# Attention backward: rings of three single PSUM banks, the dS product per head, half of one unit in four turned by TensorE and evacuated by ScalarE

## The chip, the cores and the metric

One core of a Trainium2 chip runs the whole kernel. The metric is device time in microseconds; for the kernel before it is the median of three runs. The engines are TensorE (PE; its weight loads are shown as PEld), VectorE (DVE), ScalarE (ACT), GpSimd (POOL) and SyncE (SP, which here only issues DMA). Matmul results land in PSUM, which has eight banks of 512 fp32 a partition; DVE and ACT read them out.

## The reference, cut to what matters

A transformer block (layer norm with modulation, attention with 32 heads of width 16 over 2048 positions, an MLP with squared ReLU) is run forward and backward: the outputs are the block's output and the gradients of nine inputs. The part that matters is the gradient of the attention:

```python
q, k, v = (qkv[0], qkv[1], qkv[2])            # H = 32, Dh = 16, S = 2048
scores = jnp.einsum('bhqd,bhkd->bhqk', q, k) * scale
p = _softmax(scores, axis=-1)
o = jnp.einsum('bhqk,bhkd->bhqd', p, v)
...
_out, _vjp = jax.vjp(_f, A_x, A_wqkv, A_wo, B_w1, B_b1, B_w2, B_b2, c, w_mod)
_grads = _vjp(grad_out)
```

With P the probabilities and dO the gradient of o, the backward pass needs dP = dO V^T, dS = P * (dP - rowsum(dO * O)), then dV = P^T dO, dK = dS^T Q and dQ = dS K. The scores are computed again, block by block. The row sums and the division by the softmax's sums are folded into the operands earlier, so that in the loop below dS is one product of dP (in PSUM) and the exponential (in SBUF).

## The kernel before: the attention backward loop

The kernel has a forward stage, this loop, and a last stage with the weight gradients. The loop goes over 8 groups of four heads (`g`), two pairs of heads in each (`jp`), four chunks of 512 keys (`c`) and 16 blocks of 128 queries (`ib`): 1024 units. A unit is one block of queries against one chunk of keys for two heads (`a` = 0 and 1). Units come in fours (G), which share one SBUF tile `ds`.

The eight PSUM banks: two for score tiles (`st`), two tiles of two banks each for dP (`dp`), one accumulator for dK and dV (`acckv`), one for dQ (`accq`).

```python
stp = es.enter_context(tc.tile_pool(name="p5st", bufs=2, space=PSUM))
dpp = es.enter_context(tc.tile_pool(name="p5dp", bufs=2, space=PSUM))
accp = es.enter_context(tc.tile_pool(name="p5acc", bufs=1, space=PSUM))
```

Work on a unit is spread over time. In step i the scores of unit i and the dP of the unit before are multiplied in turn, head by head; the exponential follows per head, the dS product for both heads at once:

```python
for a in range(2):
    stt = stp.tile([P, 512], F32, name="st")
    rs = slice(64 * jp, 64 * jp + 64)
    nc.tensor.matmul(stt[:], lhsT=T["QT"][rs, q], rhs=masked["KT"][2 * jp + a][rs, c0:c0 + 512],
                     start=True, stop=True)
    if last:
        dP(dp, last, a)
    nc.scalar.activation(pu[:, a, :], stt[:], ACT.Exp, scale=self.scale)
if last:
    dS(dp, last)
last = (T, g, jp, c, ib, kvT, pu, dsg, i, grp)
if i % 2 == 1 and len(pend) >= 4:
    r = kv_two()                       # dK, dV of two earlier units
    if r:
        turnq.append(r)
elif i % 2 == 0 and len(pendq) > 2 * G:
    for _ in range(4 if len(pendq) > 3 * G else 2):
        dq(pendq.pop(0), [0, 1])       # dQ of two earlier units
if i == G - 1 and ib0 // G % 2:
    turn_ds(dsg, grp)
```

`dq` needs dS transposed (`dsT`, 32 blocks of 128x128 for four units). A DMA does that when the four units are complete, issued from SP:

```python
def dS(dp, u):
    (T, g, jp, c, ib, kvT, pu, dsg, i, grp) = u
    nc.vector.tensor_tensor(dsg[:, i], dp[:], pu[:], ALU.mult)
    pend.append((T, g, jp, c, ib, kvT, pu, dsg[:, i]))
    if i == G - 1:
        i0 = len(grp)
        dsT = grp[0] if i0 else dtp.tile([P, 8 * G, P], BF16, name="dsT")
        nc.sync.dma_start_transpose(dsT[:, 8 * i0:, :], dsg[:, i0:].rearrange("p i a k -> p (i a k)"))
        for i in range(G):
            pendq.append((T, g, jp, c, ib - G + 1 + i, i, dsT))
```

In every second group of four units the first unit's eight blocks go another way: TensorE transposes them into a score tile, ACT copies half of it out and DVE the other half. The DMA then has 24 blocks to do.

```python
def turn_ds(dsg, grp):
    dsT = dtp.tile([P, 8 * G, P], BF16, name="dsT")
    tp = stp.tile([P, 8, P], BF16, name="st")
    for b in range(8):
        nc.tensor.transpose(tp[:, b, :], dsg[:, 0, b // 4, b % 4 * P:(b % 4 + 1) * P], self.ident[:])
    nc.scalar.copy(dsT[:, 0:4, :], tp[:, 0:4, :])
    nc.vector.tensor_copy(dsT[:, 4:8, :], tp[:, 4:8, :])
    grp.append(dsT)
```

`kv` runs four matmuls for each unit into `acckv`, on four strips of columns; after the sixteenth block DVE moves the sums to `kvT`. At the end of a pair of heads `turn` transposes `kvT` in 16 blocks, in a `dp` tile, and ACT copies the result out.

Of the kernel before, what the change touches and what calls it, by code (L numbers as in the profile page):

```python
# [8 lines left out]
BF16 = mybir.dt.bfloat16  # L9
F32 = mybir.dt.float32  # L10
ACT = mybir.ActivationFunctionType
ALU = mybir.AluOpType
AX = mybir.AxisListType
PSUM = bass.MemoryType.PSUM
# [4 lines left out]
P = 128  # L19
DH = 16  # L20
# [67 lines left out]
class K:  # L88
# [1070 lines left out]
    def attn_bwd(self):  # L1159
# [7 lines left out]
        tc, nc = self.tc, self.nc  # L1167
        S, D, H, NQ, ST, SC = self.S, self.D, self.H, self.NQ, self.ST, self.SC
        G = 4
        W = 4 * DH  # L1170
        with ExitStack() as es:
            dtp = es.enter_context(tc.tile_pool(name="p5dt", bufs=4))
            kvp = es.enter_context(tc.tile_pool(name="p5kv", bufs=1))
            stp = es.enter_context(tc.tile_pool(name="p5st", bufs=2, space=PSUM))
            dpp = es.enter_context(tc.tile_pool(name="p5dp", bufs=2, space=PSUM))
            accp = es.enter_context(tc.tile_pool(name="p5acc", bufs=1, space=PSUM))
            acckv = accp.tile([P, 512], F32, name="acckv")
            nc.vector.memset(acckv[:], 0.0)
# [4 lines left out]
            def kv(u):  # L1183
                (T, g, jp, c, ib, kvT, pu, ds) = u
                for j, (n, src) in enumerate((("Q", ds), ("dO", pu))):
                    for a in range(2):
                        r = 64 * j + 32 * a
                        col = (2 * jp + a) * DH
                        nc.tensor.matmul(acckv[r:r + DH, :], lhsT=T[n][:, ib, col:col + DH], rhs=src[:, a, :],  # L1189
                                         start=(ib == 0), stop=(ib == ST - 1))  # L1190
                if ib == ST - 1:
                    nc.vector.tensor_scalar(kvT[:, 512 * c:512 * (c + 1)], acckv[:], kvs[:], None, ALU.mult)

            def turn(g, jp, kvT):
                h0 = 4 * g + 2 * jp
                tp = dpp.tile([P, ST, P], BF16, name="dp")
                for st in range(ST):
                    nc.tensor.transpose(tp[:, st, :], kvT[:, st * P:(st + 1) * P], self.ident[:])
                v = tp[:].rearrange("p s (t a e) -> p t s a e", t=2, a=2)
                for t, dst in enumerate((self.dk_t, self.dv_t)):  # L1200
                    d = dst[:, :, h0 * DH:(h0 + 2) * DH].rearrange("p s (a d) -> p s a d", a=2)
                    nc.scalar.copy(d, v[:, t, :, :, 0:DH])

            def dq(u, heads):
# [13 lines left out]
            def kv_two():  # L1218
                for u in pend[:2]:
                    kv(u)  # L1220
                (T, g, jp, c, ib, kvT, pu, ds) = pend[1]
                del pend[:2]
                return (g, jp, kvT) if c == SC - 1 and ib == ST - 1 else None

            def dP(dp, u, a):
                (T, g, jp, c, ib, kvT, pu, dsg, i, grp) = u
                rd = slice(64 - 64 * jp, 128 - 64 * jp)
                nc.tensor.matmul(dp[:, a, :], lhsT=T["dOT"][rd, ib * P:(ib + 1) * P],  # L1228
                                 rhs=masked["VT"][2 * jp + a][rd, 512 * c:512 * (c + 1)], start=True, stop=True)

            def dS(dp, u):
                (T, g, jp, c, ib, kvT, pu, dsg, i, grp) = u
                nc.vector.tensor_tensor(dsg[:, i], dp[:], pu[:], ALU.mult)  # L1233
                pend.append((T, g, jp, c, ib, kvT, pu, dsg[:, i]))
                if i == G - 1:
                    i0 = len(grp)
                    dsT = grp[0] if i0 else dtp.tile([P, 8 * G, P], BF16, name="dsT")
                    nc.sync.dma_start_transpose(dsT[:, 8 * i0:, :], dsg[:, i0:].rearrange("p i a k -> p (i a k)"))
                    for i in range(G):
                        pendq.append((T, g, jp, c, ib - G + 1 + i, i, dsT))  # L1240

            def turn_ds(dsg, grp):

                dsT = dtp.tile([P, 8 * G, P], BF16, name="dsT")
                tp = stp.tile([P, 8, P], BF16, name="st")
                for b in range(8):
                    nc.tensor.transpose(tp[:, b, :], dsg[:, 0, b // 4, b % 4 * P:(b % 4 + 1) * P], self.ident[:])
                nc.scalar.copy(dsT[:, 0:4, :], tp[:, 0:4, :])
                nc.vector.tensor_copy(dsT[:, 4:8, :], tp[:, 4:8, :])
                grp.append(dsT)  # L1250

            T = self.T0
            turnq, last = [], None
            for g in range(NQ):
                for jp in range(2):
                    pieces = []
                    if jp == 0:
                        pieces = self.pair_pieces(g, 1)
                    elif g + 1 == NQ:
                        for st in range(0, ST, 2):  # L1260
                            pieces.append((self.xhat1_6[:, st:st + 2, :], self.xhat1_d.rearrange("(st p) d -> p st d", p=P)[:, st:st + 2, :]))
                        for kt in range(self.DT):
                            pieces.append((self.wq_6[:, kt, :], self.io["A_wqkv"][kt * P:(kt + 1) * P, :]))
                    else:
                        Tn, pieces = self.load_group(g + 1)
                        pieces = self.pair_pieces(g + 1, 0) + pieces
                    kvT = kvp.tile([P, S], BF16, name="kvT")
                    for c in range(SC):
                        c0 = 512 * c
                        for ib0 in range(0, ST, G):  # L1270
                            if pieces and (c or ib0):
                                nc.sync.dma_start(*pieces.pop(0))
                            dsg, grp = self.dsp.tile([P, G, 2, 512], BF16, name="ds"), []
                            for i in range(G):
                                ib = ib0 + i
                                q = slice(ib * P, (ib + 1) * P)
                                if turnq and i == 2:
                                    turn(*turnq.pop(0))
                                pu = self.pup.tile([P, 2, 512], BF16, name="pu")

                                if last:
                                    dp = dpp.tile([P, 2, 512], F32, name="dp")
                                for a in range(2):
                                    stt = stp.tile([P, 512], F32, name="st")
                                    rs = slice(64 * jp, 64 * jp + 64)
                                    nc.tensor.matmul(stt[:], lhsT=T["QT"][rs, q], rhs=masked["KT"][2 * jp + a][rs, c0:c0 + 512],  # L1286
                                                     start=True, stop=True)
                                    if last:
                                        dP(dp, last, a)
                                    nc.scalar.activation(pu[:, a, :], stt[:], ACT.Exp, scale=self.scale)  # L1290
                                if last:
                                    dS(dp, last)
                                last = (T, g, jp, c, ib, kvT, pu, dsg, i, grp)
                                if i % 2 == 1 and len(pend) >= 4:
                                    r = kv_two()
                                    if r:
                                        turnq.append(r)
                                elif i % 2 == 0 and len(pendq) > 2 * G:
                                    for _ in range(4 if len(pendq) > 3 * G else 2):
                                        dq(pendq.pop(0), [0, 1])  # L1300
                                if i == G - 1 and ib0 // G % 2:
                                    turn_ds(dsg, grp)
                T = Tn
            dp = dpp.tile([P, 2, 512], F32, name="dp")
            for a in range(2):
                dP(dp, last, a)
            dS(dp, last)
            while len(pend) > 2:
                kv_two()
            turn(*kv_two())  # L1310
            while pendq:
                dq(pendq.pop(0), [0, 1])

# [253 lines left out]
```

The softmax here doesn't subtract the row's maximum and nothing guards it: scores larger than these inputs give would overflow.

## Time and profile before

| | |
|---|---|
| time | 2849.95 us (2847.93 to 2849.98, three runs) |
| span of the profile | 2845.7 us |
| first exponential of the backward loop | at 1256.2 us |
| last dS product starts | at 2703.6 us |
| PE, DVE, ACT busy over the span | 91%, 64%, 81% |
| exponential, 128x512 | 2048 times, 596 ns |
| dS product, 128x1024 | 1024 times, 1218 ns |
| ACT's copy of turned dS, 128x512 | 128 times, 585 ns |
| DVE's copy of turned dS, 128x512 | 128 times, 424 ns |
| DVE's move of dK and dV sums (`kvT`) | 64 times, 741 ns |
| transposing DMA, issue to landing | 256 times, 6.8 us in the median |

A row of groups in the profile reads: source line, engine, operation, output tile and input tiles with their shapes, count, then busy time, mean length of one in ns, and the idle time of the engine just before them with what ended it. Instructions of one engine overlap a little, so busy time is less than count times length. A timeline gives start and length in us; consecutive instructions of a kind are merged with their count. The backward loop is a steady repetition, so one cycle of it shows what costs time in all of them.

### The profile page before, as it was taken

To read this page: it belongs to the slowest core of one execution; us is meant where nothing else is said; L and a number is where in the kernel's file an instruction comes from. 1 tells how busy PE (TensorE), PEld (TensorE's weight loads), DVE (VectorE), ACT (ScalarE), POOL (GpSimd) and SP (SyncE) were. 2 spreads that over 40 slices of the span, in tenths; PEclk is the share of its full clock that TensorE was granted. 3 is DMA by queue.
4 is the path that set the end of the run, shared out by engine and by line. 5 is a ranking of instruction groups with operands and counts; after the bars stand their busy time and mean duration, and the time that the engine had idled before them with its cause. 6 is when DMAs were issued, how large, how long until landed. Compare 5 with 4: busy or idle time off the path is not lost. (4 is left out here: it accounts for less than half of the span.)

```text
span 2845.7 us, 74675 instructions
## 1 busy us (share of the span) xinstructions
PE 2590.2 (91%) x31210; PEld 1280.3 (45%) x31210; DVE 1830.7 (64%) x2840; ACT 2293.5 (81%) x3504; POOL 365.0 (13%) x639
## 2 busy tenths in 40 slices
PE   5999899999999989979989998999999899999997
PEld 2555455555555545724434443444444434444443
DVE  4222323323413345649988898889988899888957
ACT  4999899999999965238888888888888888888823
POOL 2244201310311123420000000000000000000031
PEclk9999999999999999989999999999999999999999
DMA  4367632520531266989999999999999999999986
GB/s 150 88 147 161 167 78 83 128 66 28 135 90 50 86 156 176 194 193 169 193 172 175 189 171 193 172 171 195 168 193 175 170 194 168 189 179 172 209 219 165
DMA packets 1198010, 439.45 MB, mean 154 GB/s; under 512 B 1135430, under 2 KB 1159496, under 8 KB 1197672
## 3 DMA queue, kind: packets, MB, share of 16 engines
q1 hardware_dynamic: 1165608, 342.70, 64.4%
q0 software_dynamic: 29952, 89.36, 10.8%
q8 instruction: 244, 4.00, 0.6%
q10 hardware_dynamic: 2112, 2.62, 0.3%
q14 instruction: 94, 0.77, 0.1%
HBM read 83.30 MB, written 67.11 MB: 53 GB/s over the span
## 5 line engine op out<-in xcount | busy, mean ns | idle before, releaser
L1290 ACT ACTIVATE pu<-st 128x512 bf16<-128x512 f32 x2048 | 1125.6, 596 | 210.0 <-PE dp L1228 115.7
L1233 DVE TENSOR_TENSOR ds<-dp,pu 128x1024 bf16<-128x1024 f32 x1024 | 1204.0, 1218 | 112.1 <-PE dp L1228 83.7
L331 ACT ACTIVATE pu<-st 128x1024 bf16<-128x1024 f32 x1024 | 956.1, 1046 | 22.6 <-PE st L328 21.0
L328 PE MATMUL st<-QTm,KTq 128*128 128x512 bf16 x2048 | 611.6, 380 | 30.5 <-ACT pu L331 7.7
L293 PEld LDWEIGHTS <-pu 128*128 128x128 bf16 x8192 | 345.2, 96 | 249.6 <-issue 24.8
L1286 PE MATMUL st<-m,q 64*128 64x512 bf16 x1024 | 362.7, 382 | 68.2 <-ACT pu L1290 61.1
L1286 PE MATMUL st<-m,QTq 64*128 64x512 bf16 x1024 | 361.2, 380 | 63.7 <-ACT pu L1290 56.8
L1228 PE MATMUL dp<-m,q 64*128 64x512 bf16 x1024 | 364.3, 387 | 0.0
L293 PE MATMUL accbank<-Vaug,pu 128*128 128x17 bf16 x8192 | 349.1, 171 | 15.0 <-DVE O L301 13.4
L1228 PE MATMUL dp<-m,dOTq 64*128 64x512 bf16 x1024 | 362.4, 384 | 0.0
L1209 PEld LDWEIGHTS <-dsT 128*128 128x128 bf16 x8192 | 239.2, 96 | 133.5 <-issue 127.5
L328 PEld LDWEIGHTS <-KTq 128*128 128x128 bf16 x2048 | 194.2, 96 | 205.6 <-issue 140.5
L1340 POOL DMA_DIRECT2D O_tm<-O_d x2 | 1.8, 913 | 1458.0 <-PE accq L1209 1458.0
L1228 PEld LDWEIGHTS <-q 64*128 64x128 bf16 x1024 | 94.1, 93 | 176.5 <-issue 168.3
L1228 PEld LDWEIGHTS <-dOTq 64*128 64x128 bf16 x1024 | 94.2, 92 | 166.9 <-issue 158.5
L1189 PE MATMUL acckv<-ds,Qg 128*16 128x512 bf16 x1024 | 154.0, 381 | 0.6 <-DVE ds L1233 0.6
L1189 PE MATMUL acckv<-ds,q 128*16 128x512 bf16 x1024 | 154.5, 382 | 0.0
L1189 PE MATMUL acckv<-pu,q 128*16 128x512 bf16 x1024 | 154.5, 382 | 0.0
L1189 PE MATMUL acckv<-pu,dOg 128*16 128x512 bf16 x1024 | 154.0, 381 | 0.0
L1209 PE MATMUL accq<-Kg,dsT 128*128 128x16 bf16 x4096 | 142.8, 170 | 3.2 <-DMA dsT<-ds 3.2
L1209 PE MATMUL accq<-q,dsT 128*128 128x16 bf16 x4096 | 143.5, 170 | 0.8 <-DMA dsT<-ds 0.8
L300 DVE RECIPROCAL rl<-accbank 128x4 f32<-128x4 f32 x128 | 22.9, 179 | 167.5 <-PE accbank L293 167.2
(314 smaller groups left out, 2643.5 us busy)
## 6 DMA issues: line engine op xcount, KB each, us to landing
KTq<-KTq_d POOLq DMA_DIRECT2D x24, 512.0 KB, 3.8
duT_d<-auT POOLq DMA_DIRECT2D x4, 1792.0 KB, 8.2
aT_d<-rT POOLq DMA_DIRECT2D x4, 1792.0 KB, 13.2
KTq_d<-KTq SPq DMA_DIRECT2D x32, 128.0 KB, 1.9
QTq_d<-ev_fm SPq DMA_DIRECT2D x32, 128.0 KB, 2.0
VTq_d<-vT POOLq DMA_DIRECT2D x4, 1024.0 KB, 6.4
O_d<-O POOLq DMA_DIRECT2D x4, 1024.0 KB, 7.4
m<-KTq_d SPq DMA_DIRECT2D x32, 128.0 KB, 2.9
```

The source lines that it names most:

```text
L293: nc.tensor.matmul(acc[:, a, sub, :], lhsT=pu[:, a, sub * P:(sub + 1) * P], rhs=Vaug[:, kb, h, :], start=(kb == 0 and a == 0 and sub == 0) ...
L300: nc.vector.reciprocal(self.rl[:, st0:st0 + 4, h], acc[:, a, :, DH])
L328: nc.tensor.matmul(stt[:, a, :], lhsT=KT[:, kb * P:(kb + 1) * P], rhs=QTm[2 * jp + a][:], start=True, stop=True)
L331: nc.scalar.activation(pu[:], stt[:], ACT.Exp, scale=self.scale)
L1189: nc.tensor.matmul(acckv[r:r + DH, :], lhsT=T[n][:, ib, col:col + DH], rhs=src[:, a, :], start=(ib == 0), stop=(ib == ST - 1))
L1209: nc.tensor.matmul(accq[:, ib, a, :], lhsT=dsT[:, (i * 2 + a) * 4 + sub, :], rhs=T["K"][:, 4 * c + sub, col:col + DH], start=(c == 0 and i ...
L1228: nc.tensor.matmul(dp[:, a, :], lhsT=T["dOT"][rd, ib * P:(ib + 1) * P], rhs=masked["VT"][2 * jp + a][rd, 512 * c:512 * (c + 1)], start=Tru ...
L1233: nc.vector.tensor_tensor(dsg[:, i], dp[:], pu[:], ALU.mult)
L1286: nc.tensor.matmul(stt[:], lhsT=T["QT"][rs, q], rhs=masked["KT"][2 * jp + a][rs, c0:c0 + 512], start=True, stop=True)
L1290: nc.scalar.activation(pu[:, a, :], stt[:], ACT.Exp, scale=self.scale)
L1340: nc.gpsimd.dma_start(O_tm[:, b, :], tm_v(self.O_d)[:, b, :])
```

## The change

The score tiles get a ring of three single banks instead of two. The dP tiles become single banks as well, one for each head, in a ring of three, instead of two tiles of two banks. That again is six banks. The dS product is done per head, right after that head's dP. TensorE now transposes only the first head of the first unit (four blocks, half a bank), but in every group of four units, so the DMA has 28 blocks each time; ACT alone copies them out. They are issued in the third step of the group instead of the fourth. The turning of `kvT` is split in two parts of eight blocks, which use score tiles. The purpose is that a transposition should hold back neither the scores nor DVE, and that DVE is freed of copies. The results are the same.

The diff, cut to its core:

```diff
-            stp = es.enter_context(tc.tile_pool(name="p5st", bufs=2, space=PSUM))
-            dpp = es.enter_context(tc.tile_pool(name="p5dp", bufs=2, space=PSUM))
+            stp = es.enter_context(tc.tile_pool(name="p5st", bufs=3, space=PSUM))
+            dpp = es.enter_context(tc.tile_pool(name="p5dp", bufs=3, space=PSUM))
...
-            def turn(g, jp, kvT):
+            def turn(g, jp, kvT, s0):
                 h0 = 4 * g + 2 * jp
-                tp = dpp.tile([P, ST, P], BF16, name="dp")
-                for st in range(ST):
-                    nc.tensor.transpose(tp[:, st, :], kvT[:, st * P:(st + 1) * P], self.ident[:])
+                n = ST // 2
+                tp = stp.tile([P, n, P], BF16, name="st")
+                for st in range(n):
+                    nc.tensor.transpose(tp[:, st, :], kvT[:, (s0 + st) * P:(s0 + st + 1) * P], self.ident[:])
...
-            def dP(dp, u, a):
+            def dP(u, a):
                 (T, g, jp, c, ib, kvT, pu, dsg, i, grp) = u
                 rd = slice(64 - 64 * jp, 128 - 64 * jp)
-                nc.tensor.matmul(dp[:, a, :], lhsT=T["dOT"][rd, ib * P:(ib + 1) * P],
+                dp = dpp.tile([P, 512], F32, name="dp")
+                nc.tensor.matmul(dp[:], lhsT=T["dOT"][rd, ib * P:(ib + 1) * P],
                                  rhs=masked["VT"][2 * jp + a][rd, 512 * c:512 * (c + 1)], start=True, stop=True)
-            def dS(dp, u):
+                nc.vector.tensor_tensor(dsg[:, i, a], dp[:], pu[:, a, :], ALU.mult)
+
+            def dS(u):
                 (T, g, jp, c, ib, kvT, pu, dsg, i, grp) = u
-                nc.vector.tensor_tensor(dsg[:, i], dp[:], pu[:], ALU.mult)
...
-                    i0 = len(grp)
-                    dsT = grp[0] if i0 else dtp.tile([P, 8 * G, P], BF16, name="dsT")
-                    nc.sync.dma_start_transpose(dsT[:, 8 * i0:, :], dsg[:, i0:].rearrange("p i a k -> p (i a k)"))
+                    dsT = grp[0]
+                    nc.sync.dma_start_transpose(dsT[:, 4:, :], dsg[:].rearrange("p i a k -> p (i a k)")[:, 512:])
...
-                tp = stp.tile([P, 8, P], BF16, name="st")
-                for b in range(8):
-                    nc.tensor.transpose(tp[:, b, :], dsg[:, 0, b // 4, b % 4 * P:(b % 4 + 1) * P], self.ident[:])
-                nc.scalar.copy(dsT[:, 0:4, :], tp[:, 0:4, :])
-                nc.vector.tensor_copy(dsT[:, 4:8, :], tp[:, 4:8, :])
+                tp = stp.tile([P, 4, P], BF16, name="st")
+                for b in range(4):
+                    nc.tensor.transpose(tp[:, b, :], dsg[:, 0, 0, b * P:(b + 1) * P], self.ident[:])
+                nc.scalar.copy(dsT[:, 0:4, :], tp[:])
...
-                                        turnq.append(r)
+                                        turnq.extend((*r, s0) for s0 in (0, ST // 2))
...
-                                if i == G - 1 and ib0 // G % 2:
+                                if i == 2:
                                     turn_ds(dsg, grp)
```

More of the change, by code (lines that the diff above doesn't have):

```diff
@@ L1192, in kv @@
                     nc.vector.tensor_scalar(kvT[:, 512 * c:512 * (c + 1)], acckv[:], kvs[:], None, ALU.mult)
-            def turn(g, jp, kvT):
+            def turn(g, jp, kvT, s0):
                 h0 = 4 * g + 2 * jp
-                tp = dpp.tile([P, ST, P], BF16, name="dp")
-                for st in range(ST):
-                    nc.tensor.transpose(tp[:, st, :], kvT[:, st * P:(st + 1) * P], self.ident[:])
+                n = ST // 2
+                tp = stp.tile([P, n, P], BF16, name="st")
+                for st in range(n):
+                    nc.tensor.transpose(tp[:, st, :], kvT[:, (s0 + st) * P:(s0 + st + 1) * P], self.ident[:])
                 v = tp[:].rearrange("p s (t a e) -> p t s a e", t=2, a=2)
                 for t, dst in enumerate((self.dk_t, self.dv_t)):
-                    d = dst[:, :, h0 * DH:(h0 + 2) * DH].rearrange("p s (a d) -> p s a d", a=2)
+                    d = dst[:, s0:s0 + n, h0 * DH:(h0 + 2) * DH].rearrange("p s (a d) -> p s a d", a=2)
                     nc.scalar.copy(d, v[:, t, :, :, 0:DH])
@@ L1279, in attn_bwd @@
                                 pu = self.pup.tile([P, 2, 512], BF16, name="pu")
-                                if last:
-                                    dp = dpp.tile([P, 2, 512], F32, name="dp")
                                 for a in range(2):
@@ L1288, in attn_bwd @@
                                     if last:
-                                        dP(dp, last, a)
+                                        dP(last, a)
                                     nc.scalar.activation(pu[:, a, :], stt[:], ACT.Exp, scale=self.scale)
                                 if last:
-                                    dS(dp, last)
+                                    dS(last)
                                 last = (T, g, jp, c, ib, kvT, pu, dsg, i, grp)
@@ L1300, in attn_bwd @@
                                         dq(pendq.pop(0), [0, 1])
-                                if i == G - 1 and ib0 // G % 2:
+                                if i == 2:
                                     turn_ds(dsg, grp)
                 T = Tn
-            dp = dpp.tile([P, 2, 512], F32, name="dp")
             for a in range(2):
-                dP(dp, last, a)
-            dS(dp, last)
+                dP(last, a)
+            dS(last)
             while len(pend) > 2:
                 kv_two()
-            turn(*kv_two())
+            r = kv_two()
+            for s0 in (0, ST // 2):
+                turn(*r, s0)
             while pendq:
```

## The prediction

> **What bounds the kernel now.** I read the page first: busy shares, the slices, the costliest groups. Then the windows, to separate the stage that is changed from the rest; then the timeline of single engines in one cycle of that stage; then the waits.
>
> ```profile
> L1290 ACT ACTIVATE pu<-st 128x512 bf16<-128x512 f32 x2048 | 1125.6, 596 | 210.0 <-PE dp L1228 115.7
> L1233 DVE TENSOR_TENSOR ds<-dp,pu 128x1024 bf16<-128x1024 f32 x1024 | 1204.0, 1218 | 112.1 <-PE dp L1228 83.7
> ```
>
> ```profile
> 1256.20:2704.80 1448.60, 1313.64 (x17546) 580.65 (x17546) 1301.88 (x1230) 1201.69 (x2206) 0.00 (x0) 1.00 0.99 180
> ```
>
> The first two rows are groups of the page: 1024 units, each with two exponentials and one dS product of 1218 ns. The last line is a row of the windows (stretch, length, then busy time of PE, PEld, DVE, ACT, POOL, then clock, DMA share, GB/s), laid from the first exponential to the end of the last dS product. Only this stretch, 1448.6 us or 1.415 us a unit, is touched; the rest, about 1401 us, should stay. In it no engine is full: DVE is busy 1301.9 us (90%), ACT 1201.7 (83%), PE 1313.6 (91%, ends modelled). The answer must be in the waits.
>
> The next lines are the DVE timeline (start, length, count, and in brackets the idle time before), two cycles of eight units:
>
> ```profile
> 2144.51 4.60 DVE L1233 TENSOR_TENSOR ds<-dp,pu 128x1024 bf16<-128x1024 f32 x4
> 2149.24 0.43 DVE L1249 COPY dsT<-st 128x512 bf16<-128x512 bf16 x1
> 2150.20 9.62 DVE L1233 TENSOR_TENSOR ds<-dp,pu 128x1024 bf16<-128x1024 f32 x8 [0.54 <-PE dp L1228]
> 2160.22 0.42 DVE L1249 COPY dsT<-st 128x512 bf16<-128x512 bf16 x1 [0.40 <-ACT dsT L1248]
> 2161.36 4.82 DVE L1233 TENSOR_TENSOR ds<-dp,pu 128x1024 bf16<-128x1024 f32 x4 [0.72 <-PE dp L1228]
> ```
>
> Around each transposition on TensorE DVE waits for ACT's half of the evacuation (0.40), copies its own half (0.42), and then waits 0.54 to 0.72 for dP. Why dP is late stands in the PE timeline of the first of these:
>
> ```profile
> 2147.96 0.62 PE L1247 MATMUL st<-ident,ds 128*128 128x128 bf16 x8
> 2148.51 0.39 PE L1286 MATMUL st<-m,q 64*128 64x512 bf16 x1
> 2148.52 0.39 PE L1228 MATMUL dp<-m,q 64*128 64x512 bf16 x1
> 2149.76 0.37 PE L1286 MATMUL st<-m,q 64*128 64x512 bf16 x1 [0.85 <-ACT pu L1290]
> 2149.76 0.39 PE L1228 MATMUL dp<-m,q 64*128 64x512 bf16 x1
> ```
>
> The eight blocks take one of the two score buffers. The second score matmul after them needs that buffer, and PE stands 0.85 us. The page names ACT, but the DVE copy ended at 2149.24+0.43=2149.67 and PE starts 0.09 later: the copy is the last reader. DVE then starts 0.44 after the dP matmul. The waits over the stretch agree:
>
> ```profile
> PE st L1286 <- ACT pu L1290: 117.9, 150, 3.6
> ...
> DVE ds L1233 <- PE dp L1228: 83.7, 144, 1.1
> ...
> DVE dsT L1249 <- ACT dsT L1248: 30.4, 81, 0.4
> ...
> PEld L1209 <- DMA dsT<-ds: 2.9, 5, 0.9
> PE accq L1209 <- DMA dsT<-ds: 1.4, 4, 0.6
> ```
>
> PE lost 117.9 us in 150 waits, about one for each of 128 transpositions. DMA holds PE 4.3 us in all.
>
> **What the Trainium skill says.** (1) "VectorE: DVE Perf Modes", section "The perf-mode tier table": a tensor_tensor with an fp32 PSUM operand runs at one element a cycle, so halving an instruction halves only the streaming part. The trace agrees: 1218 ns for 1024 elements against 691 for 512 (the dw product of another stage), 1.03 ns an element and about 165 ns that don't shrink. (2) "Perfetto Trace Analysis", section "Optimization Strategy": the same gap repeating on the engine that should be full can mean too few buffers. That is the 0.85 us gap above. (3) The same page, "What 'DMA-bound' means": a DMA sequencer that is solid can bind by issue alone. It isn't solid here, but see the third rival.
>
> **The change, part by part, per eight units** (now 1448.6/128 = 11.32 us).
>
> *DVE work.* What counts is the distance from start to start, less than the length because instructions overlap. Four dS products in 4.60 us with the last 1.22 long: (4.60-1.22)/3 = 1.13. For half products I take two 512-element tensor_tensors from PSUM that stand back to back in an earlier stage of the DVE timeline:
>
> ```profile
> 1192.73 0.69 DVE L826 TENSOR_TENSOR dw<-dps,mod 128x512 bf16<-128x512 f32 x1 [1.05 <-PE dps L823]
> 1193.34 0.68 DVE L829 TENSOR_TENSOR g2w<-dps,w_blk 128x512 f32<-128x512 f32 x1
> ```
>
> They start 0.61 apart (0.60 in another such pair). Sixteen halves: 16x0.605 = 9.68, against 8x1.13 = 9.04: the split costs 0.64. The copy of 0.42 goes (about 0.38 by distance). kvT stays: 0.65 in every second cycle, 0.33; dq 0.08. DVE without any wait: before 9.04+0.38+0.33+0.08 = 9.83, after 9.68+0.33+0.08 = 10.09. So DVE does slightly more work, and the gain can only come from the 11.32-9.83 = 1.49 us of loss in a cycle.
>
> *The loss.* Around a transposition it is the waits above: in the first cycle 0.13+0.54, in the second 0.40+0.72, mean about 0.9. The rest, about 0.6, is spread over products that start 1.2 apart rather than 1.13 (9.62 for eight) and over the turns at the end of each pair.
>
> *What the rings change.* Transposition now fills half a bank, one of three score slots, read by ACT alone. The next two score matmuls use the other slots; the slot itself is needed again two scores and a burst of other matmuls later (at least 1.1 us), while ACT's copy takes 0.585. So the 0.85 us stop should vanish, and DVE's wait for ACT with it. For dP: half n may be written once the product of half n-3 is done, so PE has two products, 1.21 us, to deliver. Alone it needs 0.09+0.44 = 0.53 us (the two latencies above). The tight case is a burst between dP n and dP n+1. From the end of product n-3: 0.09 to dP n, 0.32 to the burst (the usual gap in the PE timeline), 0.50 of dq, 0.30 of four transposes, 0.44 from dP n+1 to its product, together 1.65; DVE gets to product n+1 after three products, 1.81. It just fits. I keep 0.4 of the 1.49 us for stops like these, for the turns and for jitter among four engines that are all nearly full.
>
> *ACT.* Exponentials are 0.524 apart ((2.17-0.597)/3 in a row of four): 16x0.524 = 8.38, two copies at 0.49 apart 0.98 (one before), turns 0.12: 9.48 against DVE's 10.09. Not the bound, if it doesn't stand idle waiting for the transposes; with three slots scores can lie ready so that ACT has other work then.
>
> *PE.* Unblocked, a pair of units shows gaps 0.23+0.32 (scores and dP, twice), 0.50 (dq), 0.54 (kv): 2.14 us, so 8.56 in eight units, plus eight transposes as before 0.6 and turns 0.15: 9.3.
>
> *DMA.* 24+32 blocks in two groups become 28+28: the same.
>
> *Sum.* 10.09+0.4 = 10.5 us for eight units, 128 of them: 1342 us for the stretch, 107 less than now. 2849.95-107 = 2743 us.
>
> **The rivals.**
>
> 1. *Three half-size dP buffers are too few.* Before there were four halves' worth, in two units. If PE's bursts (dq and transposes together, 0.8 us, once in four units) starve DVE each time by 0.3 to 0.5 us, that is 0.6 to 1.0 in eight units, and the cycle is 11.0 to 11.3: 2810 to 2847 us. For it: the slack above is only 0.16 us. Against: it assumes PE arrives at the burst as late as the ring allows, and PE has 0.8 us to spare in a cycle.
>
> 2. *ACT becomes the bound.* It waits for the transposes 128 times now (50.0 us, 0.39 each). With 256 transpositions and the same wait: 9.48+0.78 = 10.26 us, a little above DVE's own 10.09. Together with waits for scores it could reach 10.8: 2780 us. Against: these waits occur with two slots, where ACT can't be behind; with a backlog they cover themselves.
>
> 3. *The transposing DMA becomes the bound.* In the timeline of SP its issue takes 4.79 us for 32 blocks and 3.59 for 24, 0.15 a block: 4.19 for 28, and 0.57 more with about 0.1 of gap where a load is issued in between. That is 4.86 in a group of four units; DVE alone needs 5.05. The share of 0.99 in the windows speaks for it, the 4.3 us of PE waits and the idle issue queue between transposes against. Loads in a third of the groups stretch the issue to over 5 us, so it may cost some 15 us; if it is the real limit, the cycle is about 10.8: 2780 us.
>
> 4. *Better than thought:* no loss but DVE's own work, 10.1: 2692 us.
>
> **Range and chances.** My 2743 lies between rival 4 (2692) and rivals 2 and 3 (2780). Rival 1 is the one that brings it near no gain. I set 2700 to 2805 for 8 in 10. Faster by over 2% means below 2793: 0.82. Within 2%: 0.15, if rival 1 is half true. Slower by over 2%: 0.03, since every engine's own sum stays below the present cycle.
>
> **What would show each step.** Half products: 2048 of about 690 ns and some 0.60 apart in unbroken rows; if the distance is above 0.65, the DVE term is wrong. The stop of PE on scores (117.9 us) should be nearly gone, and so should DVE's wait for dP where it follows a transposition. DVE should be busy over 94% of the stretch, and the stretch some 1340 us. If ACT is above 95% and DVE waits for pu, rival 2 holds; if PE waits for dsT, rival 3; if DVE still waits for dP by tens of us, rival 1. The prediction is wrong in its core if the 0.85 us stop goes and the stretch doesn't shrink with it.

## The result and the profile after

| | before | changed | ratio (95% interval) |
|---|---|---|---|
| time, us | 2848.94 | 2729.0 (2719.86 to 2732.09) | 0.957 (0.9545 to 0.9593) |
| span of the profile, us | 2845.7 | 2718.1 | |
| loop, start of the first exponential to start of the last dS product, us | 1447.4 | 1328.3 | |

The profiled run is the fastest of the four. Its loop is 119.1 us shorter. The rest of the 127.6 us by which the spans differ lies ahead of the loop, where nothing was changed and where its start moves by up to 14 us from kernel to kernel (1248 to 1262 us). After the loop 142.1 and 141.7 us are left.

The rows of the page's groups for the two main lines after the change (busy time, mean ns, idle time before and what ended most of it), and the page's ACT copy of turned dS:

```profile
L1234 DVE TENSOR_TENSOR ds<-dp,pu 128x512 bf16<-128x512 f32 x2048 | 1242.0, 679 | 44.3 <-PE dp L1232 36.4
L1290 ACT ACTIVATE pu<-st 128x512 bf16<-128x512 f32 x2048 | 1074.4, 607 | 137.4 <-PE dp L1232 103.3
...
L1252 ACT COPY dsT<-st 128x512 bf16<-128x512 bf16 x256 | 151.3, 591 | 2.1 <-PE st L1251 1.9
```

The windows over the loop (PE, PEld, DVE, ACT, POOL busy, then clock, DMA share, GB/s):

```profile
1248.10:2577.10 1329.00, 1262.61 (x17546) 524.44 (x17546) 1286.19 (x2126) 1201.30 (x2364) 0.00 (x0) 0.99 1.11 196
```

DVE is busy 1286.2 of 1329 us, 97% against 90% before. ACT no longer waits for transposes (2.1 us for 256 copies; 50.0 for 128 before). DVE's wait for dP has fallen from 83.7 to 36.4 us.

Two stretches of the DVE timeline show where the rest lies. The first is from the first half of a group of heads, the second from a second half, in which the loads for the next group stand in a row:

```profile
1604.93 19.21 DVE L1234 TENSOR_TENSOR ds<-dp,pu 128x512 bf16<-128x512 f32 x32
1624.06 0.74 DVE L1192 TENSOR_SCALAR kvT<-acckv,kvs 128x512 bf16<-128x512 f32 x1
1624.72 19.21 DVE L1234 TENSOR_TENSOR ds<-dp,pu 128x512 bf16<-128x512 f32 x32
```

```profile
2055.17 3.68 DVE L1234 TENSOR_TENSOR ds<-dp,pu 128x512 bf16<-128x512 f32 x6 [0.84 <-PE dp L1232]
2058.77 0.74 DVE L1192 TENSOR_SCALAR kvT<-acckv,kvs 128x512 bf16<-128x512 f32 x1
2059.43 1.27 DVE L1234 TENSOR_TENSOR ds<-dp,pu 128x512 bf16<-128x512 f32 x2
2062.07 2.48 DVE L1234 TENSOR_TENSOR ds<-dp,pu 128x512 bf16<-128x512 f32 x4 [1.36 <-PE dp L1232]
```

In the first, DVE has no gap at all: 16 units take 1624.72-1604.93 = 19.79 us. If all 64 such pieces ran so, the loop would take 64x19.79 plus 10 for dQ, 1276 us. It takes some 52 more, and nearly all of that in the second halves: from first product to first product the eight of them take 683.1 us, the eight first halves 644.6. The PE timeline of the second stretch says why dP was late there:

```profile
2054.27 0.46 PE L1211 MATMUL accq<-q,dsT 128*128 128x16 bf16 x12 [1.11 <-DMA dsT<-ds]
...
2061.16 0.46 PE L1211 MATMUL accq<-q,dsT 128*128 128x16 bf16 x12 [2.21 <-DMA dsT<-ds]
```

PE stands in front of dQ until the DMA has landed, and the scores and dP that follow it in the program stand behind it (the next score matmul starts at 2061.55). The waits of the loop have three lines that matter now:

```profile
PEld L1211 <- DMA dsT<-ds: 44.4, 38, 2.7
PE accq L1211 <- DMA dsT<-ds: 40.6, 35, 2.6
...
PE dp L1232 <- DVE ds L1234: 21.1, 50, 0.5
```

PE and its weight loads wait for the same transposes (the first two lines are one wait, seen twice): some 41 us, against 1.4 before (the prediction's 4.3 adds up such a pair of lines). So the old stop is gone, DVE is full wherever DMA keeps up, and DMA is what now takes time elsewhere.

### The profile page after: what moved, and what is told of

Read it like the earlier page. It is cut to its first block, busy times and chain, and to the rows that moved or that the text cites. A ratio compares the mean times of both kernels' runs of the same rounds, so it can differ in the third digit from the quotient of the medians.

```text
span 2718.1 us, 76855 instructions
## 1 busy us (share of the span) xinstructions
PE 2531.8 (93%) x31210; PEld 1220.6 (45%) x31210; DVE 1814.3 (67%) x3736; ACT 2293.1 (84%) x3664; POOL 367.4 (14%) x639
## 5 line engine op out<-in xcount | busy, mean ns | idle before, releaser
L1234 DVE TENSOR_TENSOR ds<-dp,pu 128x512 bf16<-128x512 f32 x2048 | 1242.0, 679 | 44.3 <-PE dp L1232 36.4
L1290 ACT ACTIVATE pu<-st 128x512 bf16<-128x512 f32 x2048 | 1074.4, 607 | 137.4 <-PE dp L1232 103.3
L1232 PE MATMUL dp<-m,dOTq 64*128 64x512 bf16 x1024 | 347.1, 384 | 11.7 <-DVE ds L1234 11.7
L1232 PE MATMUL dp<-m,q 64*128 64x512 bf16 x1024 | 347.9, 386 | 10.3 <-DVE ds L1234 9.4
L1286 PE MATMUL st<-m,q 64*128 64x512 bf16 x1024 | 317.8, 386 | 4.0 <-ACT pu L1290 2.3
L1286 PE MATMUL st<-m,QTq 64*128 64x512 bf16 x1024 | 316.2, 384 | 1.6
L1252 ACT COPY dsT<-st 128x512 bf16<-128x512 bf16 x256 | 151.3, 591 | 2.1 <-PE st L1251 1.9
L274 POOL DMA_DIRECT2D QTm<-QTq_d x126 | 63.6, 508 | 387.9 <-PE st L328 378.7
```

What stands on the lines that cost most here:

```text
L274: nc.gpsimd.dma_start(QTm[j][32 * j:32 * j + 32, :], self.QTq_d[g, 32 * j:32 * j + 32, 512 * qc:512 * (qc + 1)])
L1232: nc.tensor.matmul(dp[:], lhsT=T["dOT"][rd, ib * P:(ib + 1) * P], rhs=masked["VT"][2 * jp + a][rd, 512 * c:512 * (c + 1)], start=True, sto ...
L1234: nc.vector.tensor_tensor(dsg[:, i, a], dp[:], pu[:, a, :], ALU.mult)
L1252: nc.scalar.copy(dsT[:, 0:4, :], tp[:])
```

## The experiments

Theory at the start: a transposition on TensorE cost time by holding one of only two score slots; the third slot removes that, the single copier makes it cheap, and what is lost now is DMA in the halves with loads. Rivals: the DVE copies were the cost; the dP ring matters, not the scores'; PE or ACT is as close as DVE; DMA is full everywhere. Each kernel is timed against the kernel before on the same chip, and ratios are to that; loops are from the profiles, first exponential to last product.

**1. The new transposition alone** (two score banks, two double dP banks and whole products, as before):

```diff
-                    nc.sync.dma_start_transpose(dsT[:, 8 * i0:, :], dsg[:, i0:].rearrange(...))
+                    nc.sync.dma_start_transpose(dsT[:, 4:, :], dsg[:].rearrange(...)[:, 512:])
-                for b in range(8): ...            # ACT copies 4 blocks, DVE copies 4
+                for b in range(4): ...            # ACT copies all
-                                if i == G - 1 and ib0 // G % 2:
+                                if i == 2:
```

> The kernel before with the new transposition alone: four blocks in every group of four units, in its third step, copied out by ACT only. Two score banks, two dP tiles of two banks and whole dS products stay. Theory (a transposition costs by holding one of only two score slots): the stop of PE on scores stays, about 0.3 to 0.5 us each, but now 256 times; DVE's own work falls to 9.45 us in eight units (no copy, no split), the cycle is about 10.8 us, 2770 to 2800 us. Rival A (it was the DVE copies and their waits, the rings add nothing): all of the gain, about 2730 us or less. Rival B (the gain is all in the rings): no gain, about 2850 us.

Measured: 2845.3 us, 0.997 (0.996 to 0.999); loop 1441.7. Almost nothing, though DVE was rid of 128 copies. ACT, DVE and PE around one group of four units:

```profile
2101.82 2.14 ACT L1288 ACTIVATE pu<-st 128x512 bf16<-128x512 f32 x4 [0.28 <-PE dp L1228]
2104.24 1.08 ACT L1288 ACTIVATE pu<-st 128x512 bf16<-128x512 f32 x2 [0.28 <-PE dp L1228]
2105.31 0.58 ACT L1247 COPY dsT<-st 128x512 bf16<-128x512 bf16 x1
2105.79 1.16 ACT L1288 ACTIVATE pu<-st 128x512 bf16<-128x512 f32 x2
```

```profile
2101.04 4.77 DVE L1233 TENSOR_TENSOR ds<-dp,pu 128x1024 bf16<-128x1024 f32 x4 [0.51 <-ACT pu L1288]
2106.46 4.76 DVE L1233 TENSOR_TENSOR ds<-dp,pu 128x1024 bf16<-128x1024 f32 x4 [0.65 <-ACT pu L1288]
```

```profile
2102.95 0.37 PE L1284 MATMUL st<-m,q 64*128 64x512 bf16 x1
...
2103.50 0.38 PE L1189 MATMUL acckv<-pu,q 128*16 128x512 bf16 x2
...
2103.82 0.39 PE L1284 MATMUL st<-m,q 64*128 64x512 bf16 x1
```

The reader should see two things. Away from the transposition, four exponentials and a gap of 0.28 take 2104.24-2101.82 = 2.42 us: 1.21 us a unit, longer than the 1.13 that DVE needs for a whole product. (The gap is put down to dP, whose matmul starts and ends with that of the score.) The second of the four exponentials ends at about 2102.93 and so frees a slot; PE fills it at 2102.95, then is in its burst for dK and dV until 2103.82, and only then comes the score for which ACT waits at 2104.24. With a third slot PE could have filled it before and been through the burst earlier. And each transposition still costs DVE 0.65 us, now twice in eight units and through the exponential (156.6 us in all), where before it waited longer, but once. So with two score slots a closed loop of score, exponential and score again sets the pace, and freeing DVE is worth nothing. Both the theory's size and rival A fell; rival B came nearest, though the rings alone don't bring all of the gain either (experiment 2).

**2. The rings and half products alone** (with the old transposition, the first edit undone in the changed kernel).

> The changed kernel with the old transposition: eight blocks in every second group, ACT and DVE each copy half. Rings of three single banks and products per head stay. Theory: the stop of PE on scores is gone also here, since the slot is needed again only after two scores and a burst; DVE pays its copy (0.38 us in eight units) and its wait for ACT (0.2 to 0.4), so the cycle is about 10.9 us, 2780 to 2805 us. Rival A (copies are all of it): about 2850 us. Rival B (rings are all of it): within 10 us of the changed kernel, 2729 us.

Measured: 2783.2 us, 0.976 (0.973 to 0.978); loop 1384.7. As the theory had it. With experiment 1 this makes a table of loops:

| loop, us | two score slots, whole products | three and three, halves |
|---|---|---|
| old transposition | 1447.4 | 1384.7 |
| new transposition | 1441.7 | 1328.3 |

The rings (with their halves) alone bring 62.7 us, the transposition alone 5.7, both 119.1: 50.7 us of the gain are in neither part alone. The new transposition is worth 56.4 us once there are three slots. By the timeline most of that is DVE's copy, which costs 0.33 us from start to start where DVE has work waiting, 42 us for 128 of them (DVE with the old transposition and the new rings):

```profile
1614.19 0.41 DVE L1254 COPY dsT<-st 128x512 bf16<-128x512 bf16 x1
1614.52 1.88 DVE L1234 TENSOR_TENSOR ds<-dp,pu 128x512 bf16<-128x512 f32 x3
```

So taking copies from DVE was worth next to nothing while the score slots set the pace, and counts once DVE does. No run moves the copy alone, so this share is a sum and not a measurement.

**3 and 4. Six banks shared out otherwise**: in the changed kernel, two score slots and four for dP halves; then four and two.

```diff
-            stp = ... name="p5st", bufs=3 ...        # 2 | 4
-            dpp = ... name="p5dp", bufs=3 ...        # 4 | 2
```

> The changed kernel with the six banks shared out as two for scores and four for dP halves. Theory (the third score slot is what removes the stop): the stop of PE on scores comes back at 256 transpositions by 0.3 to 0.5 us, partly covered by the deeper dP ring: 2750 to 2790 us. Rival (three dP halves are too few, the dP ring limits): faster than 2729 us, by up to 20 us.

> The changed kernel with the six banks shared out as four for scores and two for dP halves. Theory (a product for half n frees the slot for half n+2, so PE has one product's time, 0.6 us, and every burst of dQ or dK/dV matmuls of 0.5 us starves DVE): PE and DVE wait for each other by hundreds of us, 2900 us or more. Rival (scores are all that matters): within 20 us of the changed kernel.

Measured: 2826.8 us with two score slots, 0.991 (0.989 to 0.993), loop 1424.5; 2872.9 us with two dP slots, 1.008 (1.006 to 1.010), loop 1474.5; three and three: 1328.3. Each ring needs its third slot. The first lies beyond the theory's range, the second short of it. With two score slots ACT shows the gaps of experiment 1 again, and PE waits for a slot that ACT still copies at almost each transposition (a line of the waits, then ACT's timeline over one group of four units):

```profile
PE st L1286 <- ACT dsT L1252: 52.7, 255, 0.3
```

```profile
2100.98 2.14 ACT L1290 ACTIVATE pu<-st 128x512 bf16<-128x512 f32 x4 [0.28 <-PE dp L1232]
2103.40 1.08 ACT L1290 ACTIVATE pu<-st 128x512 bf16<-128x512 f32 x2 [0.28 <-PE dp L1232]
...
2106.39 2.14 ACT L1290 ACTIVATE pu<-st 128x512 bf16<-128x512 f32 x4 [0.28 <-PE dp L1232]
```

PE's waits are only half of what this kernel loses (96 us). Two units without a transposition take 2103.40-2100.98 = 2.42 us, about what DVE needs for their four halves (4x0.598 = 2.39); the two with it take 2106.39-2103.40 = 2.99. The loop of two slots has no slack in which ACT's copy could hide, and pays it in every group; the theory counted PE's own stop alone. With two dP slots the waits are between PE and DVE, both ways, as the theory said, if smaller than it said:

```profile
DVE ds L1234 <- PE dp L1232: 88.1, 261, 0.8
PE dp L1232 <- DVE ds L1234: 35.9, 186, 0.5
```

**5. The split alone**: the kernel before with two products of 512 in place of one of 1024.

```diff
-                nc.vector.tensor_tensor(dsg[:, i], dp[:], pu[:], ALU.mult)
+                for a in range(2):
+                    nc.vector.tensor_tensor(dsg[:, i, a], dp[:, a, :], pu[:, a, :], ALU.mult)
```

> The kernel before with the dS product split in two instructions of 512 elements; nothing else. If the split costs what two adjacent instructions of an earlier stage said (0.605 against 1.13/2 us from start to start, 0.64 us in eight units) and the stops stay, the cycle goes from 11.32 to about 11.9 us: 2920 to 2940 us. Rival (a product per head starts earlier, and the stops absorb the rest): 2850 to 2870 us.

Measured: 2863.4 us, 1.004 (1.0025 to 1.005), loop 18.5 us longer. The instructions cost what was said (eight in 4.86 us), but DVE had waited anyway, as the rival had it. This too says that the kernel before wasn't bound by DVE.

**6. One more small DVE instruction per unit** in the changed kernel (a copy of 128x64 into a tile nobody reads).

> The changed kernel with one more small DVE instruction per unit (a copy of 128x64 bf16 to a scratch tile), about 0.12 us each from start to start, 123 us in 1024 units. Theory (DVE alone sets the pace in all stretches without loads): the time rises by 70 to 125 us, to 2800 to 2850 us. Rival (PE and ACT are as close, DVE has room): it rises by less than 40 us.

Measured: 2774.3 us, 0.974 (0.972 to 0.976); against 0.957 this is 45 us more. The copies take 0.08 us each from start to start (two products and a copy in 1.28 us where two products take 1.20), 82 us in all: a little over half of it shows, less than the theory had and more than the rival. It shows where the theory says: the eight first halves are 39.2 us longer, 4.9 each where 64 copies take 5.1, the second halves only 10.5 in all. DVE has hardly a gap in either now, and PE's wait for dsT has fallen from 41 to 12 us: in the halves with loads the copies only filled time that DMA took anyway. DVE alone sets the pace in the halves without loads; in the others DMA does, and only just.

**7. All of dS transposed by DMA** (no blocks on TensorE, no copies on ACT; 32 blocks instead of 28).

> The changed kernel without any transposition of dS on TensorE: DMA transposes all 32 blocks. Rings and products per head as in the changed kernel. Theory (DMA is close behind DVE): issue rises from 4.19 to 4.79 us a group, PE waits for dsT by 100 us or more in the halves with loads, 2770 to 2830 us. Rival (DMA has room; the transposition costs more than it spares): 2690 to 2730 us, since ACT loses 256 copies and PE 1024 transposes.

Measured: 2851.0 us, 1.0005 (0.9995 to 1.002). The whole gain is lost, more than the theory's range allowed. PE's wait for dsT:

```profile
PE accq L1211 <- DMA dsT<-ds: 169.2, 116, 3.4
```

The issue of a transpose on SP, in the kernel before (24 and 32 blocks in turn) and in the changed one (28): shortest, median and longest in ns:

```profile
L1238 SPq DMA_TRANSPOSE dsT<-ds x256: 3566/4766/5948, 1263.1 to 2705.2; - x128
```

```profile
L1242 SPq DMA_TRANSPOSE dsT<-ds x256: 4114/4704/6042, 1254.1 to 2577.2; - x128
```

The prediction took 0.15 us a block from two issues (4.79 and 3.59) that are among the shortest. In the mean 32 blocks took 5.07 and 24 took 3.91 before, 0.160 a block; in the changed kernel 28 take 4.65, 0.166; here 32 take 5.25, 0.164. With 120 loads of 0.67 us between the transposes (all that stand there, those for the last stage too), 0.31 in a group on average, the changed kernel's DMA needs 4.97 us a group: what DVE needs (19.79/4 = 4.95). The two are level on average, and a group with a load needs some 5.3. Part of this run's loss is PE's clock (last section).

**8 to 10. Getting around DMA**: loads issued from GpSimd, which is idle; dQ half a group later; loads spread evenly (8 and 7 in the two halves instead of 4 and 11).

```diff
-                                nc.sync.dma_start(*pieces.pop(0))
+                                nc.gpsimd.dma_start(*pieces.pop(0))            # 8
-                                elif i % 2 == 0 and len(pendq) > 2 * G:
+                                elif i % 2 == 0 and len(pendq) > 2 * G + 2:    # 9
-                            if pieces and (c or ib0):
+                            if pieces and (c or ib0) and (ib0 // G % 2 or g + 1 == NQ):   # 10
```

> The changed kernel with the loads of the next heads' operands (102 in the loop) issued from GpSimd instead of SP; the transposes stay on SP. In the changed kernel PE waits 43 us for dsT, all in the second half of each group of heads, where these loads are issued between the transposes and SP is solid. Theory (issue-bound there: 4.2 to 5.1 us a transpose plus 0.67 for a load against 4.95 us that DVE needs): freeing 0.67 us a group brings the waits below 20 us and the time to 2695 to 2715 us. Rival (bandwidth: the loads' bytes slow the transposes, whoever issues them): waits stay at 40 us or more, 2720 to 2750 us, more if the loads now come in one burst.

> The changed kernel with dQ matmuls half a group later (two more units pending before they are taken), so a transpose has about 2.5 us more until PE needs it; same instructions. Theory (the waits are a backlog that builds over the eleven groups with loads, some 4 to 5 us, against about 2.8 us of slack): PE's waits for dsT fall from 43 to under 15 us, and part of it comes back as DVE waiting for the dS tile that the DMA still reads; 2700 to 2715 us. Rival (a lasting limit of throughput in those stretches): the wait only moves, 2720 us or more.

> The changed kernel with the loads for the next heads spread over the whole group of heads: one in every second group of units, 8 in the first pair's half and 7 in the second's, instead of 4 and 11 in a row. Same loads, same bytes, still from SP. Theory (DMA's pace falls behind DVE's only where loads stand in a row; on average it needs about 4.7 us a group against 4.95): PE's waits for dsT fall from 43 to under 10 us and the time to 2675 to 2695 us. Rival (DMA is full everywhere, its share over 1 says so): waits only spread out, 2715 to 2735 us.

Measured: 2772.8 us (0.973, 0.971 to 0.975), 2721.8 (0.9555, 0.953 to 0.958) and 2718.2 (0.953, 0.951 to 0.956). From GpSimd the loads are no longer held back by the transposes between them: they go as soon as their tiles are free, several at once, one transpose's issue takes up to 17.9 us, and PE waits for dsT up to 9.9 us at a time, 68.5 in all. The second halves get shorter (659.8 us in all against 683.1), the first, into which the bursts fall, longer (710.2 against 644.6). So loads side by side hold a transpose back, and keeping them apart was of use; what issuing from GpSimd at the old pace would do is not shown. Later dQ moves the wait: PE no longer stands for dsT, but DVE waits 14.0 us for tiles that the DMA still reads, and ACT 34.4 us for transposes. Spreading leaves 38.8 us of PE waits, in both halves now. In all three the rival came nearer (DMA has no room to speak of; the first is above the rival's range, as the rival allowed for bursts), and intervals of 9 and 10 overlap the changed kernel's: neither is shown to be faster.

**11 and 12. The dK and dV sums moved by ACT**, 64 times, alone and with spread loads.

```diff
-    nc.vector.tensor_scalar(kvT[:, 512 * c:512 * (c + 1)], acckv[:], kvs[:], None, ALU.mult)
+    nc.scalar.activation(kvT[:, 512 * c:512 * (c + 1)], acckv[:], ACT.Copy, scale=kvs[:])
```

> The changed kernel with the move of the dK and dV sums (64 times, 0.65 us of DVE by distance) on ACT instead of DVE. If DVE sets the pace and ACT has the 7% of room that its busy time shows (76.4 of 82 us), the loop gets shorter by 20 to 40 us: 2690 to 2710 us. Rival (ACT then is as full as DVE was, and the accumulator is freed later because ACT comes to it later): no gain or a loss, 2725 to 2760 us.

> As the kernel with spread loads, and the move of the dK and dV sums on ACT. If the move alone gave little because DMA held the second halves, it gives 15 to 30 us more here: 2650 to 2675 us. Rival (ACT is full then): within 10 us of the kernel with spread loads.

Measured: 2719.3 us (0.954, 0.9525 to 0.956) alone, 2713.9 us (0.952, 0.951 to 0.954) with spread loads. Of 40 us taken from DVE, 13 show in the loop of the first, less than theory and more than the rival had; PE's waits for dsT rise to 52 us. Its interval overlaps the changed kernel's. For the second the rival held: it is within 10 us of the kernel with spread loads. Its median is the lowest of the study, clear of the changed kernel by about half a per cent, but not of experiments 10 and 11.

## Why the prediction was right, point by point

**Time.** 2743 was predicted, 2729 measured; the loop came out at 1328 against 1342. The steps on DVE and on the stop of PE hold; that the number is so near owes something to luck, as two points below show.

**The DVE term.** Right. Halves are (19.21-0.68)/31 = 0.598 us apart, predicted 0.605. With kvT and dQ DVE's own work is 9.97 us in eight units, predicted 10.09. That a PSUM operand keeps a tensor_tensor at one element a cycle (the Trainium skill, "VectorE: DVE Perf Modes", section "The perf-mode tier table") fits: 512 elements more cost 1.13-0.598 = 0.53 us, 1.04 ns each, and the split saves no streaming time.

**The stop on scores.** Right. PE's 117.9 us of waits for a score slot are 2.3, and DVE's copy and its wait are gone.

**The 0.4 us kept as remaining loss.** Right in size, wrong in kind. Eight units take 1328.3/128 = 10.38, so 0.41 over DVE's own work. I had named PE's stops, the turns and jitter; in the first halves there is hardly any of it (32 products without a gap), and some 45 of the 52 us are in the second halves, where PE waits for the transposing DMA. So the 51 us kept (128x0.4) for stops that came to a few us covered a DMA for which 15 had been allowed: here two errors cancel.

**What bounded the kernel before.** This step was wrong in part. I put 1.49 us in eight units down to stops around a transposition (0.9) and to a remainder. The remainder, products 1.2 us apart instead of 1.13, was seen but not explained: it was the closed loop of two score slots, 1.21 us a unit (experiment 1). The sum for the transposition alone, built without that loop, was 45 to 75 us too low. The prediction came out right because the change gives both a third slot and a cheap transposition.

**Rival 1 (dP ring).** Its arithmetic was close: three slots just suffice (PE waits 21.1 us for dP slots in the whole loop), two don't (experiment 4).

**Rival 2 (ACT).** Fell: 2.1 us of waits for transposes. Exponentials with a backlog are also closer together than I read off before: six in 3.07 us, (3.07-0.60)/5 = 0.494 apart, where the 0.524 came from rows with small waits in them.

**Rival 3 (DMA).** Undersized. I allowed 15 us; the loop loses about 45 that way. The mis-sized term is the issue time, 0.15 us a block read from issues among the shortest, where the means are 0.160 before and 0.166 after; 4.19 for 28 blocks should have been 4.65. A group with a load then needs 5.3 us instead of 4.86, more than DVE's 4.95, and a row of eleven such groups builds up a backlog. The Trainium skill ("Perfetto Trace Analysis", section "What 'DMA-bound' means") names the sign, an issuing sequencer that is solid with DMA. Here transposes and loads filled 84% of the loop on SP before (1220 of 1446 us) and 95% after (1262 of 1327).

## What to carry to other kernels

Where two engines pass tiles through a ring of two and the producer also has bursts of other work, the ring itself sets the pace: look for the same small gap on the consumer once in every round of bursts (0.28 us in every two units here), even when another engine is busier. A part of a change tested alone can show nothing because the other part's limit hides it, so measure both alone and together. And before speeding up a loop, work out the pace of each queue from the mean over the loop; a rate read from a few short issues is too good (0.15 us a block against 0.160 to 0.166 here).

## What was unexpected of the hardware

A stop of PE can be followed by a slow stretch. After the wait of 2.21 us at 2061.16 the score matmuls of the changed kernel took their usual 0.38 us for another 1.5 us, and then 0.6 for about three:

```profile
2061.78 0.38 PE L1286 MATMUL st<-m,q 64*128 64x512 bf16 x1
...
2064.79 0.63 PE L1286 MATMUL st<-m,q 64*128 64x512 bf16 x1
...
2066.32 0.39 PE L1286 MATMUL st<-m,q 64*128 64x512 bf16 x1
```

The granted clock was 0.50 from 2064 to 2066 us and 1.00 from 2068. The same followed a wait of 2.58 us near 1381. The Trainium skill ("TensorE: Matmul & The Clock Gate", section "What's actually happening") gives half rate after an idle window of about 3.4 us; here 2.2 us of waiting, with a wait of 1.1 us some 7 us earlier, was enough, and the measurement decides. It isn't the wait's length alone: of eleven waits of 1.8 to 2.6 us in the loop seven were followed by such a stretch within 1.7 us and four were not, a wait of 2.20 at 2033.07 among them. What tells them apart is not shown here. So a DMA wait can cost more than its own length: the clock over the loop was 0.99 in the changed kernel and 0.94 where DMA transposes everything.
